# One weight load moved up, one unit of the output product moved up, and one pair of copies shared by two engines, in an attention-plus-MLP kernel

## The chip, the cores and the metric

The kernel runs on one core of a Trainium2 chip. The metric is the device time of one execution in microseconds; less is better. The engines are TensorE (PE, with its weight loads shown as PEld), VectorE (DVE), ScalarE (ACT), GpSimd (POOL) and SyncE (SP). Each takes its own instructions in order and waits on the others through semaphores. In this kernel nearly all loads from memory are issued by POOL, into one queue of software DMAs.

## The reference, cut to what matters

Two layers follow each other. The first is attention with an exponential decay per head (4 batches, 8 heads, 768 positions, 64 wide), computed in blocks of 64 positions with a running state. The second is an MLP on its 3072 x 512 output.

```
for each block b of 64 positions:
    intra = ((q_b k_b^T) * Dmask) v_b
    inter = (q_b * lam_pow) kv_state
    out_b = intra + inter
    kv_state = lam^64 * kv_state + (k_b * rev_pow)^T v_b

h = x @ w_in                      # 512 -> 2048
g = h + sin(alpha h)^2 / alpha
y = g @ w_out                     # 2048 -> 512
```

## The kernel before, in words

The 768 positions are cut into six chunks of 128. A chunk is taken for all four batches, so that the MLP works on 512 columns at a time. The batches go through the attention in two pairs: pair 0 is batches 0 and 1, pair 1 is batches 2 and 3. The order of the instructions on every engine is written out by hand; nothing reorders them.

**The MLP of a chunk.** `hidden(g, f)` multiplies one of 16 slices of `w_in` with the chunk's `xt` (four matmuls, L507), takes the sine on ACT (L510) and its square on ACT (L515) or DVE (L523). `finish(g, f)` forms the slice of `gall` on DVE (L524), and with that the PSUM bank of the slice is free. `project(g, m, part)` is one *unit*: four matmuls (L535) that multiply a quarter of `gall` for batch m with the quarter `w_out_sb[part]`. Units wait in a list, and `run(n)` issues the next n of it. The list for the first chunk begins (0,0), (1,0), (2,0), (3,0), (0,1), (1,1), (2,1), (3,1), (0,2), and so on, as (m, part). A unit with part 3 is followed by a store; the others are matmuls alone.

**The attention of the second chunk** is woven into the MLP of the first, and then into its last units. Its steps, which the change touches, are these.

- `turns_pair(t, nm, b, bk, engines)` turns k or q of a pair on PE (L338 to L341) into PSUM bank `bk`, both batches into the same bank. Two copies, one for each batch, take it from there into `QKT` (L344 for a copy on ACT, the DVE's own line where an engine given is `V`).
- `states(t, prs, ns)` forms the new state contributions of both 64-blocks of a pair (L423), block 0 in the first bank of `ns`, block 1 in the second.
- `update(1, 0, pr)` adds block 0 to the state on DVE (L399) and lets POOL cast it (L392). `update(1, 1, pr)` adds block 1 with four small DVE instructions (L403), and POOL casts it.
- `scores(t, prs, ns)` multiplies k and q (L443); `masks` takes the result out on DVE (L450).
- `outputs_first(t, prs, ns)` begins the outputs from the states (L457), block 0 in the first bank of `ns`, block 1 in the second. Its matmuls take the two blocks by turns. `outputs` adds the part within the block (L482), and `leave` takes the result to `xt` on DVE (L489).

For pair 1 the banks meet as follows: `states(1, (1,), (4, 2))` puts block 1 into bank 2, where L403 reads it; `outputs_first(1, (1,), (4, 2))` puts its own block 1 into bank 2.

A first chunk's helper, `turn_in_two`, has a form near to the changed one. It turns one batch of q into one bank and copies the first half on ACT (L296) and the second on DVE (L297).

**The loads** of the weights are issued by POOL: `load_w_in` (L89) and `load_w_out` (L92), 512 KB each as they land. On POOL's queue w_in's quarters 1, 2 and 3 are followed by w_out's first quarter; POOL's next instructions are the two decays of k for the first chunk (L257) and the table of masks (L217), and then the loads of the second chunk's k, q and v (L104).

Of the kernel before, what the change touches and what calls it, by code (L numbers as in the profile page):

```python
# [15 lines left out]
def kernel(  # L16
# [41 lines left out]
    def bank(nm, n, dtype=FP32):  # L58
        return psum.tile([P, 512 if dtype is FP32 else 1024], dtype, name=nm, tag=f"b{n}")
# [27 lines left out]
    def load_w_in(i, w0=0, w1=512):  # L87
        w = slice(512 * i + w0, 512 * i + w1)
        nc.gpsimd.dma_start(out=w_in_sb[i][:, :, w0:w1], in_=moe_w_in[:, w].rearrange("(c p) g -> p c g", p=P))  # L89

    def load_w_out(i):
        nc.gpsimd.dma_start(out=w_out_sb[i][:],  # L92
                            in_=moe_w_out[i * 512:(i + 1) * 512, :].rearrange("(f p) d -> p f d", p=P))

    def load(t, nm, b0, b1):
        dst, src = NAT[nm]
        to = dst[t][:, b0:b1, :, :].rearrange("p b h e -> p (b h) e")
        by_head = src[b0:b1, :, t * T:(t + 1) * T, :].rearrange("b h p e -> p (b h) e")
        n = H * (b1 - b0)
        if t > 1 and nm != "v" and b0 == 2:  # L100
            nc.gpsimd.dma_start(out=to[:, 0:n - 1, :], in_=by_head[:, 1:n, :])
            nc.gpsimd.dma_start(out=to[:, n - 1:n, :], in_=by_head[:, 0:1, :])
        else:
            nc.gpsimd.dma_start(out=to, in_=by_head)  # L104
# [20 lines left out]
        nc.gpsimd.dma_start(out=vn[0][:, 3, hs, :], in_=v[3, hs, 0:T, :].rearrange("h p e -> p h e"))  # L125
    load_w_in(0, 0, 2 * P)
    load_w_in(0, 2 * P, 512)
    for i in range(1, 4):
        load_w_in(i)

    fill = consts.tile([P, 512], BF16, name="fill")
    nc.vector.memset(fill[:], 1.0)  # L132
# [3 lines left out]
    def spin(n, bk, cols=256):  # L136
        ps = bank("hps", bk)
        for _ in range(n):
            nc.tensor.matmul(out=ps[:, 0:cols], lhsT=fill[:, 0:P], rhs=fill[:, 0:cols], start=True, stop=True)  # L139
# [82 lines left out]
    V, G, A = nc.vector, nc.gpsimd, nc.scalar  # L222
# [4 lines left out]
    def turned_by_one(t, pr):  # L227
        return bool(t) and pr == 1

    def in_turn(t, pr):  # L230
        return t > 1 and pr == 1
# [11 lines left out]
    def home(t, blk):  # L243
        return SB[2 if blk else t % 2]
# [7 lines left out]
    def decay_k(t, b0, b1):  # L252
        if t not in kdec:
            kdec[t] = kdp.tile([P, B, H, D], BF16, name="kdec")
        R = later["R64" if t else "R128"]
        o = int(in_turn(t, b0 // 2))
        nc.gpsimd.tensor_tensor(out=kdec[t][:, b0:b1, :, :], in0=kn[t][:, b0:b1, :, :],  # L257
                                in1=R[:, o:o + H].unsqueeze(1).unsqueeze(3).broadcast_to([P, b1 - b0, H, D]),
                                op=ALU.mult)
# [56 lines left out]
    def turn(t, nm, b, n, eng):  # L316
        src, u = (kn, 0) if nm == "k" else (qn, 1)
        ps = bank("T_ps", n, BF16)[:].rearrange("p (n c i) -> p n c i", n=2, c=HP)[:, u]
        for hp in range(HP):
            nc.tensor.transpose(out=ps[:, hp, :], in_=src[t][:, b, 2 * hp:2 * hp + 2, :], identity=iden[:])  # L320
        if eng is nc.scalar:
            eng.copy(out=both[t][:, u, b, :, :], in_=ps)
        else:
            eng.tensor_copy(out=both[t][:, u, b, :, :], in_=ps)
# [4 lines left out]
    def turns_pair(t, nm, b, bk, engines):  # L329
        src, n = (kn, 0) if nm == "k" else (qn, 1)  # L330
        ps = bank("T_ps", bk, BF16)[:].rearrange("p (u c i) -> p u c i", u=2, c=HP)
        flat = src[t][:, b:b + 2].rearrange("p b h d -> p (b h) d")
        o = int(turned_by_one(t, b // 2) and not in_turn(t, b // 2))
        for u in range(2):
            for hp in range(HP):
                h = u * H + 2 * hp + o
                if h + 2 <= 2 * H:
                    nc.tensor.transpose(out=ps[:, u, hp, :], in_=flat[:, h:h + 2, :], identity=iden[:])  # L338
                else:
                    nc.tensor.transpose(out=ps[LO, u, hp, :], in_=flat[:, h, :], identity=iden[:])  # L340
                    nc.tensor.transpose(out=ps[HI, u, hp, :], in_=flat[:, 0, :], identity=iden[:])  # L341
        for u, eng in enumerate(engines):
            if eng is nc.scalar:
                eng.copy(out=both[t][:, n, b + u, :, :], in_=ps[:, u])  # L344
            else:
                eng.tensor_copy(out=both[t][:, n, b + u, :, :], in_=ps[:, u])
# [29 lines left out]
    def states1(t, pr, n):  # L376
        ps = bank("KV0_ps", n)[:].rearrange("p (u c d) -> p u c d", u=2, c=HP)
        for h in range(2 * H):
            half, m = where(1, pr, h)
            nc.tensor.matmul(out=ps[halves(half), m // HP, m % HP, :], lhsT=head(kdec, t, pr, h),  # L380
                             rhs=vn[t][:, 2 * pr + h // H, h % H, :], start=True, stop=True)
        new_state(1, pr, ps, "first")
# [4 lines left out]
    def decay_state(n, pr):  # L387
        nc.gpsimd.tensor_tensor(out=pair(SD, pr), in0=pair(S_of[n], pr), op=ALU.mult,  # L388
                                in1=L64[:, pr].unsqueeze(1).unsqueeze(3).broadcast_to([P, 2, HP, D]))

    def cast_state(n, pr, dst):
        nc.gpsimd.tensor_copy(out=pair(dst, pr), in_=pair(S_of[n], pr))  # L392
# [42 lines left out]
    def scores(t, prs=BOTH, ns=None):  # L435
        banks_of("F", t, prs, ns, "F_ps")
        for pr in prs:
            for u in range(2):
                for hp in range(HP):
                    for blk in range(2):  # L440
                        for hd in range(2):
                            w = halves(blk)
                            nc.tensor.matmul(out=att["F", t, pr, hd][w, u, hp, :],  # L443
                                             lhsT=KT[t][halves(hd), 2 * pr + u, hp, w],
                                             rhs=QT[t][halves(hd), 2 * pr + u, hp, w], start=True, stop=True)
# [57 lines left out]
    def hidden(g, f, between=None):  # L503
        hps = bank("hps", H0[f] if g == 0 else (0, 5, 4, 2)[f] if g == 1 and f < 4 else AB[0] if g == 1 and f == 15 else AB[f + 1] if g == 2 and f < 2 else HB[(f + 2) % 3] if g == 1 else HB[(16 * g + f + 1) % 3])
        w = w_in_sb[f // 4]
        for c in range(NDC):
            nc.tensor.matmul(out=hps[:], lhsT=w[:, c, (f % 4) * P:(f % 4 + 1) * P],  # L507
                             rhs=xt[g][:, c, :], start=(c == 0), stop=(c == NDC - 1))
        s_sb = mlps.tile([P, GRP], BF16, name="s_sb")
        nc.scalar.activation(out=s_sb[:], in_=hps[:], func=ACTF.Sin, scale=alpha_sb[:, f:f + 1])  # L510
        if between:
            between()
        s2 = mlps.tile([P, GRP], BF16, name="s2")
        if squarer(g, f) is A:
            nc.scalar.activation(out=s2[:], in_=s_sb[:], func=ACTF.Square)  # L515
        elif squarer(g, f) is G:
            nc.gpsimd.tensor_tensor(out=s2[:], in0=s_sb[:], in1=s_sb[:], op=ALU.mult)
        hps_of[g, f] = (hps, s_sb, s2)
# [99 lines left out]
    outs(0, 3, 4, None, 1)  # L618
    nc.vector.reciprocal(out=r_sb[:], in_=alpha_sb[:])
    spin(3, 3)  # L620
    load_w_out(0)
    decay_k(0, 0, 2)
    decay_k(0, 2, 4)
    mask_table()
# [25 lines left out]
    def run(n):  # L650
        for _ in range(min(n, len(behind))):
            behind.pop(0)()
# [3 lines left out]
    for f in range(NFC):  # L656
        hidden(0, f)
        if f in (1, 10):
            states1(0, f // 10, 2 if f == 10 else 4)
        if f == 10:  # L660
            decay_k(1, 0, 2)
            decay_state(1, 0)
            cast_state(1, 0, home(1, 0))
            load(1, "q", 2, 4)
            load_w_out(2)
            load_w_out(3)
            load(2, "v", 0, 2)
        if f in (11, 12):
            run(1)
        if f == 12:  # L670
            turns_pair(1, "k", 0, 4, (A, A))
        if f == 13:
            turn(1, "q", 0, 2, V)
            turn(1, "q", 1, 3, V)
        if f == 14:
            scores(1, (0,), (4, 2))
            masks(1, 0)
        if f == 15:
            run(1)
            states(1, (0,), (4, 2))  # L680
            finish(0, 14)
            update(1, 0, 0)
        if f != 14:
            finish(0, f)
# [1 line left out]
    decay_state(1, 1)  # L686
    cast_state(1, 1, home(1, 0))
    update(1, 1, 0)
    run(2)
    turns_pair(1, "k", 2, 4, (A, A))  # L690
    run(1)
    outputs_first(1, (0,), (5, 0))
# [4 lines left out]
    states(1, (1,), (4, 2))  # L697
    update(1, 0, 1)
    run(1)
    turns_pair(1, "q", 2, 5, (A, A))  # L700
    load(2, "k", 0, 2)
    run(1)
    update(1, 1, 1)
# [110 lines left out]
```

## Time and profile before

| | us |
|---|---|
| median of 3 runs (207.2 to 207.66) | 207.48 |
| the profiled execution, its own time | 207.33 |
| its span, first to last instruction | 205.6 |
| PE busy in the span | 198.1 (96%) |
| ACT busy | 143.2 (70%) |
| DVE busy | 131.5 (64%) |
| POOL busy | 106.5 (52%) |

The span is what the trace covers; 1.73 us of the execution lie outside of it. Times inside the trace count from the span's start. The granted TensorE clock was 0.999 over the span.

In the timeline a row has the start, the time, the engine, the line and operation, out<-in by the names of the program, and the count; a bracket at the end is the idle time of the engine before it and what ended it. Rows of the same kind that follow each other are merged, and a few matmul records can be missing.

### The profile page before, as it was taken

Reading aid. Unit: us, or ns where it says so; the run is one execution under the profiler, and the core shown is the slowest. Engines: PE = TensorE matmul, PEld = TensorE weight load, DVE = VectorE, ACT = ScalarE, POOL = GpSimd, SP = SyncE. Lnnn points to the kernel's source line nnn. Section 1 sums busy time; section 2 is a strip of 40 time slices with the busy share of each in tenths; the row PEclk is TensorE's granted clock in tenths of the full one; section 3 lists DMA queues with packets and bytes.
Section 4 is the critical chain, followed back from the end, with each engine's and each line's share of the span. In section 5 each row is a group of like instructions: output and inputs, shape, how many; then the busy total and the mean of one; then the engine's idle time right before and its main releaser. Section 6 shows DMA issues by size and latency. Waiting matters only on the chain.

```text
span 205.6 us, 5385 instructions
## 1 busy us (share of the span) xinstructions
PE 198.1 (96%) x2235; PEld 98.3 (48%) x2265; DVE 131.5 (64%) x219; ACT 143.2 (70%) x241; POOL 106.5 (52%) x112
## 2 busy tenths in 40 slices
PE   7999989999999999999999999999999999999994
PEld 2764445554454444445444445444445444444443
DVE  7794979473889878967556967555967544444000
ACT  7798987224999799676776666776666787887121
POOL 8999939988979975999966930002000000000000
PEclk9999999999999999999999999999999999999999
DMA  8999999999989999899999929401101101110213
GB/s 132 170 178 205 203 162 176 189 176 154 150 275 105 128 151 184 82 150 155 152 149 155 181 64 192 117 3 51 54 0 54 51 0 54 53 51 0 104 51 105
DMA packets 96683, 24.49 MB, mean 119 GB/s; under 512 B 87938, under 2 KB 94226, under 8 KB 96658
## 3 DMA queue, kind: packets, MB, share of 16 engines
q0 software_dynamic: 74528, 13.37, 86.9%
q1 hardware_dynamic: 22128, 10.76, 25.5%
q8 instruction: 18, 0.29, 0.6%
q14 instruction: 7, 0.06, 0.1%
q10 hardware_dynamic: 2, 0.00, 0.0%
HBM read 27.27 MB, written 6.29 MB: 163 GB/s over the span
## 4 chain that ended last, share of the span: by engine, by line
PE 84%; DMA 7%; POOL 6%; issue 1%; ACT 1%; POOLq 0%; ACTq 0%
PE ops L535 39%; PE hps L507 35%; DMA w_out<-in_moe_w_out_dram 7%; PE O_ps L457 2%; POOL w_in L89 2%; PE hps L560 2%; PE F_ps L443 2%; PE KV_ps L423 2%; POOL kn L104 1%; PE O_ps L482 1%; POOL vn L104 1%; PE T_ps L338 1%; POOL qn L114 1%; POOL vn L125 1%; ACT QKT L344 1%
## 5 line engine op out<-in xcount | busy, mean ns | idle before, releaser
L524 DVE SCALAR_TENSOR_TENSOR gall<-s,r_sb,hps 128x512 bf16<-128x512 bf16 x96 | 71.1, 745 | 44.5 <-ACT s L515 44.3
L507 PE MATMUL hps<-xt,w_in 128*128 128x512 bf16 x369 | 94.3, 379 | 1.1 <-issue 0.3
L535 PE MATMUL ops<-w_out,gall 128*128 128x512 bf16 x353 | 90.4, 380 | 1.7 <-DMA w_out<-in_moe_w_out_dram 0.6
L510 ACT ACTIVATE s_sb<-hps,alpha_sb 128x512 bf16<-128x512 f32 x96 | 65.2, 684 | 32.0 <-PE hps L507 31.5
L515 ACT ACTIVATE s<-s_sb 128x512 bf16<-128x512 bf16 x91 | 57.3, 630 | 2.8
L507 PEld LDWEIGHTS <-w_in 128*128 128x128 bf16 x384 | 36.6, 98 | 42.8 <-DMA w_in<-in_moe_w_in_dram 0.3
L535 PEld LDWEIGHTS <-gall 128*128 128x128 bf16 x368 | 34.6, 98 | 41.5 <-DMA w_out<-in_moe_w_out_dram 1.1
L257 POOL TENSOR_TENSOR kdec<-kn,R 128x1024 bf16<-128x1024 bf16 x12 | 22.9, 1937 | 4.2 <-DMA kn<-in_k_dram 4.1
L392 POOL CAST sb<-S 128x512 bf16<-128x512 f32 x20 | 12.3, 621 | 21.3 <-DVE S L399 21.3
L388 POOL TENSOR_TENSOR SD<-S,L 128x512 f32<-128x512 f32 x16 | 16.8, 1050 | 8.6 <-DVE S L399 8.5
L489 DVE TENSOR_TENSOR xt<-O_ps,Etab 128x512 bf16<-128x512 f32 x20 | 12.8, 684 | 6.4 <-PE O_ps L482 6.4
L104 POOL DMA_DIRECT2D vn<-in_v_dram x13 | 14.7, 1137 | 0.0
L542 DVE COPY o_sb<-ops 128x512 f32<-128x512 f32 x15 | 10.3, 689 | 4.2 <-PE ops L535 4.2
L450 DVE TENSOR_TENSOR STm<-F_ps,C 128x512 bf16<-128x512 f32 x20 | 12.8, 683 | 0.3 <-PE F_ps L443 0.3
L544 ACT COPY o_sb<-ops 128x512 f32<-128x512 f32 x8 | 4.6, 576 | 12.0 <-PE ops L535 12.0
L399 DVE TENSOR_TENSOR S<-SD,KV_ps 128x512 f32<-128x512 f32 x16 | 10.8, 683 | 0.1
L104 POOL DMA_DIRECT2D kn<-in_k_dram x9 | 10.0, 1113 | 0.4 <-issue 0.3
L344 ACT COPY QKT<-T_ps 128x512 bf16<-128x512 bf16 x8 | 4.3, 586 | 5.3 <-PE T_ps L341 5.3
L139 PE MATMUL hps<-fill 128*128 128x256 bf16 (+1 forms) x24 | 6.5, 391 | 1.4 <-DVE fill L132 1.4
L104 POOL DMA_DIRECT2D qn<-in_q_dram x6 | 7.1, 1188 | 0.0
L457 PEld LDWEIGHTS <-sb 64*64 64x64 bf16 x320 | 4.3, 108 | 4.8 <-issue 4.7
L356 DVE TENSOR_TENSOR STm<-F_ps,C 128x512 bf16<-128x512 f32 x8 | 5.2, 686 | 0.8 <-PE F_ps L352 0.4
(92 smaller groups left out, 116.8 us busy)
## 6 DMA issues: line engine op xcount, KB each, us to landing
out_dram<-o_sb SPq DMA_DIRECT2D x19, 256.0 KB, 2.4
vn<-in_v_dram POOLq DMA_DIRECT2D x10, 256.0 KB, 7.9
w_out<-in_moe_w_out_dram POOLq DMA_DIRECT2D x4, 512.0 KB, 10.8
w_in<-in_moe_w_in_dram POOLq DMA_DIRECT2D x3, 512.0 KB, 9.4
kn<-in_k_dram POOLq DMA_DIRECT2D x6, 256.0 KB, 8.7
qn<-in_q_dram POOLq DMA_DIRECT2D x6, 256.0 KB, 8.5
out_dram<-o_sb SPq DMA_DIRECT2D x8, 128.0 KB, 1.8
kn<-in_k_dram POOLq DMA_DIRECT2D x4, 240.0 KB, 6.7
```

Of the source, the lines that this page charges most:

```text
L104: nc.gpsimd.dma_start(out=to, in_=by_head)
L257: nc.gpsimd.tensor_tensor(out=kdec[t][:, b0:b1, :, :], in0=kn[t][:, b0:b1, :, :], in1=R[:, o:o + H].unsqueeze(1).unsqueeze(3).broadcast_to ...
L388: nc.gpsimd.tensor_tensor(out=pair(SD, pr), in0=pair(S_of[n], pr), op=ALU.mult, in1=L64[:, pr].unsqueeze(1).unsqueeze(3).broadcast_to([P, ...
L392: nc.gpsimd.tensor_copy(out=pair(dst, pr), in_=pair(S_of[n], pr))
L399: nc.vector.tensor_tensor(out=S, in0=pair(SD, pr), in1=ps, op=ALU.add)
L450: nc.vector.tensor_tensor(out=st[:, hd], in0=att["F", t, pr, hd], op=ALU.mult, in1=of_mask(C64, t, pr, hd).unsqueeze(1).broadcast_to([P, 2 ...
L489: nc.vector.tensor_tensor(out=xview(t)[:, 2 * pr:2 * pr + 2, blk, :, :], in0=att["O", t, pr, blk], in1=Eb, op=ALU.mult)
L507: nc.tensor.matmul(out=hps[:], lhsT=w[:, c, (f % 4) * P:(f % 4 + 1) * P], rhs=xt[g][:, c, :], start=(c == 0), stop=(c == NDC - 1))
L510: nc.scalar.activation(out=s_sb[:], in_=hps[:], func=ACTF.Sin, scale=alpha_sb[:, f:f + 1])
L515: nc.scalar.activation(out=s2[:], in_=s_sb[:], func=ACTF.Square)
L524: nc.vector.scalar_tensor_tensor(out=gall[g][:, f, :], in0=s2[:], scalar=r_sb[:, f:f + 1], in1=hps[:], op0=ALU.mult, op1=ALU.add)
L535: nc.tensor.matmul(out=ops[:], lhsT=gall[g][:, f, m * P:(m + 1) * P], rhs=w_out_sb[part][:, f % 4, :], start=(f == 0), stop=(f == NFC - 1))
```

## The change

Three edits. The load of `w_out`'s first quarter is issued ahead of `w_in`'s last quarter. After the last slice of the first chunk's MLP, two units are run ahead of the second chunk's first states where there was one, and one is run behind them where there were two. Of the two copies of the last turned q (pair 1 of the second chunk), the second is given to DVE.

```diff
     load_w_in(0, 2 * P, 512)
-    for i in range(1, 4):
-        load_w_in(i)
+    load_w_in(1)
+    load_w_in(2)
+    load_w_out(0)
+    load_w_in(3)
...
     spin(3, 3)
-    load_w_out(0)
     decay_k(0, 0, 2)
...
         if f == 15:
-            run(1)
+            run(2)
             states(1, (0,), (4, 2))
             finish(0, 14)
             update(1, 0, 0)
...
     update(1, 1, 0)
-    run(2)
+    run(1)
     turns_pair(1, "k", 2, 4, (A, A))
     run(1)
...
     update(1, 0, 1)
     run(1)
-    turns_pair(1, "q", 2, 5, (A, A))
+    turns_pair(1, "q", 2, 5, (A, V))
     load(2, "k", 0, 2)
     run(1)
     update(1, 1, 1)
     scores(1, (1,), (5, 0))
```

On the engines this makes: on POOL two neighbouring issues change places; on PE four matmuls of unit (3,0) stand ahead of the 32 of the states; on ACT one copy is gone, and on DVE a copy stands between L399 of `update(1, 0, 1)` and the four L403 of `update(1, 1, 1)`. In the changed program that copy on DVE has one wait, for the count that ACT reaches with its own copy of the pair.

## The prediction

> **What bounds the kernel now.** First the page: what is busy, and how much room there is.
>
> ```profile
> span 205.6 us, 5385 instructions
> PE 198.1 (96%) x2235; PEld 98.3 (48%) x2265; DVE 131.5 (64%) x219; ACT 143.2 (70%) x241; POOL 106.5 (52%) x112
> ```
>
> TensorE is busy for 96% of the span, so only what PE waits for can be won, and whatever makes PE wait is lost. Next, therefore, the waits of PE, all of them:
>
> ```profile
> PE hps L139 <- DVE fill L132: 1.4, 1, 1.4
> PE ops L535 <- DMA w_out<-in_moe_w_out_dram: 0.6, 1, 0.6
> PE ops L535 <- issue: 0.5, 3, 0.2
> PE hps L507 <- issue: 0.3, 2, 0.2
> PE F_ps L443 <- ACT QKT L344: 0.2, 1, 0.2
> ```
>
> Two of these are what the change touches: 0.6 us for w_out's first quarter, and 0.2 us for the copies of the last turned q. The chain that ended last tells what lies behind the first, and the timeline of PE where it falls:
>
> ```profile
> 13.50 13.73 DMA w_out<-in_moe_w_out_dram
> 27.23 0.05 issue
> ```
>
> ```profile
> 25.61 1.04 PE L507 MATMUL hps<-xt,w_in 128*128 128x512 bf16 x4
> 27.28 1.04 PE L535 MATMUL ops<-w_out,gall 128*128 128x512 bf16 x4 [0.63 <-DMA w_out<-in_moe_w_out_dram]
> 28.15 1.03 PE L507 MATMUL hps<-xt,w_in 128*128 128x512 bf16 x4
> 29.88 0.61 PE L338 MATMUL T_ps<-iden,kn 128*128 128x128 bf16 x8
> 31.19 0.61 PE L320 MATMUL T_ps<-iden,qn 128*128 128x128 bf16 x8
> ```
>
> The load was issued at 13.50 and landed at 27.23; PE went on 0.05 later. Slices and units follow each other every 0.87 us (27.28 to 28.15), so the unit would have begun at 25.61 + 0.87 = 26.48. The wait is worth 27.28 - 26.48 = 0.80 us; the 0.63 in brackets counts from the end of the pipelined matmul. After that PE waits for nothing to the end of the span but the 0.2 and the few gaps of "issue", so a shift in this stretch reaches the end of the kernel whole.
>
> **Edit 1, the loads.** What stands in the queue ahead of w_out and behind it, from POOL's timeline, and the time from issue to landing of each, from the view of the DMAs:
>
> ```profile
> 12.77 0.84 POOL L89 DMA_DIRECT2D w_in<-in_moe_w_in_dram  x1
> 19.18 1.26 POOL L104 DMA_DIRECT2D kn<-in_k_dram  x1
> 20.39 1.20 POOL L104 DMA_DIRECT2D qn<-in_q_dram  x1
> ```
>
> ```profile
> w_in<-in_moe_w_in_dram POOLq DMA_DIRECT2D x1, 512.0 KB, 11.2
> kn<-in_k_dram POOLq DMA_DIRECT2D x1, 256.0 KB, 9.7
> qn<-in_q_dram POOLq DMA_DIRECT2D x1, 256.0 KB, 10.3
> ```
>
> The landings are 12.77 + 11.2 = 23.97 for w_in's last quarter, 27.23 for w_out's first, 19.18 + 9.7 = 28.88 for the second chunk's k and 20.39 + 10.3 = 30.69 for its q. They come in the order of issue. On POOL the two issues change places and nothing else is passed, so I let the two places keep their landings: w_out at 23.97, long before 26.48, and w_in at 27.23. That one is wanted by the slice that begins at 28.15, now 28.15 - 0.80 = 27.35: hidden by 0.12.
>
> Then what is late next. The k turn moves to 29.88 - 0.80 = 29.08, and k is there at 28.88. The q turn would move to 31.19 - 0.80 = 30.39, but q lands at 30.69 whatever PE does; with the same 0.05 it starts at 30.74. So the stall does not vanish. Of 0.80 us, 0.35 turn up again at q, and the gain past that point is 31.19 - 30.74 = 0.45.
>
> **Edit 2, the unit.** The next places in question, on PE and on DVE:
>
> ```profile
> 33.84 1.03 PE L535 MATMUL ops<-w_out,gall 128*128 128x512 bf16 x4
> 34.80 0.45 PE L423 MATMUL KV_ps<-vn,kdec 64*64 64x64 bf16 x32
> 35.18 1.90 PE L535 MATMUL ops<-w_out,gall 128*128 128x512 bf16 x8
> 36.91 0.55 PE L338 MATMUL T_ps<-iden,kn 128*128 128x128 bf16 x7
> ```
>
> ```profile
> 33.45 1.28 DVE L450 TENSOR_TENSOR STm<-F_ps,C 128x512 bf16<-128x512 f32 x2
> 35.36 0.69 DVE L399 TENSOR_TENSOR S<-SD,KV_ps 128x512 f32<-128x512 f32 x1
> ```
>
> The same matmuls in another order cost PE nothing. The states need the banks that the masks free: before at 33.45 + 1.28 = 34.73, with the states at 34.80, so with both 0.45 earlier they would still meet. The moved unit puts 0.87 between them: states at 34.80 - 0.45 + 0.87 = 35.22, done at 35.67. L399 can start at 35.72 and ends at 36.41, where it ended at 36.05 before. It frees bank 4 for the second k turn, which stands at 36.91 - 0.45 = 36.46, just as 36.41 + 0.05 comes. The slack is gone, and I take 0.03 off. Gain so far 0.42, edit 2 alone worth 0 (bounds -0.05 and +0.05). POOL's cast waits for L399, so it and the load behind it come up to 0.36 later. What hangs on these loads first is the third chunk's decay of k on POOL, and the states behind it on PE:
>
> ```profile
> 50.64 3.92 POOL L257 TENSOR_TENSOR kdec<-kn,R 128x1024 bf16<-128x1024 bf16 x2 [0.92 <-DMA kn<-in_k_dram]
> 56.31 0.73 PE L423 MATMUL KV_ps<-vn,kdec 64*64 64x64 bf16 x64
> ```
>
> The decay ends at 50.64 + 3.92 = 54.56, 1.75 before the states, which covers the 0.36; without that cover it would be lost on PE.
>
> **Edit 3, the copies.** First a form of it that the kernel already has, `turn_in_two`, from the timelines of ACT and DVE; then the place itself on ACT, DVE and PE, with the mean of one copy on ACT (586 ns), and a turned copy on DVE with the row after it.
>
> ```profile
> 6.76 0.37 ACT L296 COPY QKT<-T_ps 128x256 bf16<-128x256 bf16 x1 [0.27 <-PE T_ps L295]
> 7.17 0.29 DVE L297 COPY QKT<-T_ps 128x256 bf16<-128x256 bf16 x1 [0.59 <-ACT QKT L296]
> ```
>
> ```profile
> 42.48 1.07 ACT L344 COPY QKT<-T_ps 128x512 bf16<-128x512 bf16 x2 [3.00 <-PE T_ps L341]
> L344 ACT COPY QKT<-T_ps 128x512 bf16<-128x512 bf16 x8 | 4.3, 586 | 5.3 <-PE T_ps L341 5.3
> 31.95 0.42 DVE L324 COPY QKT<-T_ps 128x512 bf16<-128x512 bf16 x1
> 32.33 0.42 DVE L523 TENSOR_TENSOR s<-s_sb 128x512 bf16<-128x512 bf16 x1
> 42.68 1.12 DVE L403 SCALAR_TENSOR_TENSOR S<-S,L,KV_ps 128x128 f32<-128x128 f32 x4
> 43.60 0.45 PE L443 MATMUL F_ps<-QKT 64*64 64x64 bf16 x32 [0.20 <-ACT QKT L344]
> 43.88 0.67 PE L457 MATMUL O_ps<-QKT,sb 64*64 64x64 bf16 x31
> ```
>
> Two engines that copy out of one bank do not work side by side here: DVE sat idle for 0.59 and began at 7.17, 0.04 after ACT's copy was done (6.76 + 0.37 = 7.13). The changed program has the same wait on the new copy. So the halves run one after the other, as they do on ACT alone now, and the new wait stands at the head of DVE's queue. Behind it are the four L403, and behind those the masks.
>
> In times, with the gain of 0.42: ACT's copy from 42.48 - 0.42 = 42.06 to 42.65 (0.59 for one), DVE's from 42.69 to 43.11. The scores can start at 43.16, 0.44 earlier than 43.60; this alone would be a small gain over two copies on ACT. But L403 starts 0.38 after DVE's copy (31.95 to 32.33), at 43.07, where it started at 42.68; with 1.12 it ends at 44.19. L403 reads bank 2, and the second matmul of `outputs_first` writes bank 2. Now L403 ends at 42.68 + 1.12 = 43.80 and the outputs start at 43.88, with no idle time. After the change they would be due 0.28 behind the scores (43.60 to 43.88), at 43.44, and have to wait to 44.19 + 0.05 = 44.24: a new wait of 0.80 on PE, and a start 0.36 later than now. Against the gain of 0.42 edit 3 costs 0.78.
>
> The Trainium skill speaks against this edit: "PSUM — Partial Sum Buffer", section "PSUM bank collisions raise a hardware error", says that accesses of two engines to one bank in the same partitions, reads included, have to be kept apart by a semaphore. The trace agrees, by the 0.59. Its section "Specifications (TRN2)" lets ScalarE and VectorE read PSUM in parallel as long as the banks differ; by that, with a bank for each half, the sum would be that of the last rival below, and no run here shows it.
>
> **The sum.** -0.42 + 0.78 = +0.36 us. Against the profiled execution's 207.33 that is 207.69; the median of the runs stands 0.15 higher, at 207.48, and the forecast for a median is 207.48 + 0.36 = 207.84, 0.17% slower. About 0.2%, or 0.41 us, is what a measurement of this kernel can tell from no change.
>
> **The rivals.** *The early load gains less.* With g for the gain at the second q turn, the time changes by 0.78 - g, as the outputs then hang on ACT's copy. g is at most 0.45 by q's landing, and every place with little room (w_in's 0.12, k's 29.08 against 28.88, bank 4's 0.00) can only take from it; a w_in or q that lands 0.45 late in the other order leaves nothing. For it speaks that the margins are so thin, against it that the queue has been at work without a break and moves the same bytes. At g = 0 it is 207.48 + 0.78 = 208.26. From g below 0.37 on the change is measurably slower.
>
> *The outputs do not wait for L403.* The trace of before shows no such wait, only that the outputs began 0.08 after L403 was done. If bank 2 did not hold them up, PE would keep the gain of the scores, 0.42 to 0.44, and the time would be 207.48 - 0.42 = 207.06, faster. It decides once L403 ends later than 43.39. Against it is the code: the same bank number in `states` and `outputs_first`.
>
> *The halves run side by side.* DVE's copy then starts with ACT's at 42.06, and the outputs at 42.06 + 0.38 + 1.12 + 0.05 = 43.61, 0.27 earlier than 43.88: 207.48 - 0.27 = 207.21. Against it are the 0.59 and the wait in the program; for it only that the first form could have waited for something else.
>
> **The numbers.** The forecast's case, g between 0.25 and 0.45, has 0.62; it gives 207.81 to 208.01. Because all the thin margins work one way, I put 0.36 of it above 207.89 and 0.26 below. The small gain has 0.18, all slower; no wait for L403 has 0.10, faster; side by side has 0.10, within. That is faster 0.10, same 0.36, slower 0.54: the likeliest time lies just inside the bound, the weight just outside of it. The range goes from 207.2, where side by side ends, to 208.3 for g = 0 with the price of edit 3 a little high; left out is the case that is faster. The likeliest case's own range is 207.8 to 208.0.
>
> **What would show it.** Right: no wait of PE for w_out; in its place one of about 0.35 for q's load ahead of L320, with the turn at 30.74; DVE's new copy idle before it, released by ACT's copy at about 42.65; PE idle for some 0.8 ahead of L457, put down to DVE's L403; everything after 44 later by 0.36. Wrong: if w_in takes w_out's place among the waits, edit 1 failed; if DVE's copy starts with ACT's, the halves overlap; if L457 follows the scores without idle time, bank 2 was no bound. A wait anywhere behind 50 would mean that I missed a consumer.

## The result, and the profile after

| | before | after |
|---|---|---|
| median, us (7 runs each) | 207.48 | 208.20 |
| range of the runs | 207.15 to 207.82 | 207.97 to 208.65 |
| profiled execution, its own time | 207.33 | 208.3 |
| its span | 205.6 | 206.4 |

The change makes the kernel slower: the ratio is 1.0035, with a 95% interval of 1.0022 to 1.0048, or +0.72 us by the medians. The forecast was 207.84. Direction, wait and place came as predicted; the size is that of the first rival with no gain at all from edits 1 and 2 (208.26). One execution of edit 3 alone, at a granted clock of 0.759 (258.72 us), and one of the last kernel below (1012.11 us) count in no ratio here. Line numbers are each kernel's own: those named in the prediction, but for the loads, are two higher in after (the units are L537 for L535, the updates L405 for L403, the outputs L459 for L457), and a few kernels below have others again, so the names of out<-in are the safer guide.

First the page of after: what is busy.

```profile
span 206.4 us, 5385 instructions
PE 198.6 (96%) x2235; PEld 98.2 (48%) x2265; DVE 132.2 (64%) x220; ACT 142.6 (69%) x240; POOL 106.7 (52%) x112
```

Nothing shows here but one copy that went from ACT (241 instructions before, 240 now) to DVE (219 before, 220 now). The waits of PE in after tell more (in total, times, longest):

```profile
PE O_ps L459 <- DVE S L405: 0.6, 1, 0.6
PE ops L537 <- issue: 0.5, 3, 0.2
PE hps L509 <- issue: 0.3, 2, 0.2
PE ops L537 <- DVE gall L526: 0.2, 1, 0.2
PE F_ps L445 <- DVE QKT L348: 0.2, 1, 0.2
```

The 0.6 for w_out is gone, and a 0.6 ahead of the outputs from the states stands in its place. There is one wait that no step of the prediction named: 0.2 for `gall`. The timeline of PE in after, at the places that the prediction followed:

```profile
26.74 1.03 PE L537 MATMUL ops<-w_out,gall 128*128 128x512 bf16 x4
27.60 1.03 PE L509 MATMUL hps<-xt,w_in 128*128 128x512 bf16 x4
...
29.77 1.03 PE L509 MATMUL hps<-xt,w_in 128*128 128x512 bf16 x3
30.92 0.62 PE L322 MATMUL T_ps<-iden,qn 128*128 128x128 bf16 x8
...
33.75 1.89 PE L537 MATMUL ops<-w_out,gall 128*128 128x512 bf16 x8 [0.22 <-DVE gall L526]
35.57 0.45 PE L425 MATMUL KV_ps<-vn,kdec 64*64 64x64 bf16 x32
...
36.87 0.55 PE L340 MATMUL T_ps<-iden,kn 128*128 128x128 bf16 x7
...
43.69 0.45 PE L445 MATMUL F_ps<-QKT 64*64 64x64 bf16 x32 [0.17 <-DVE QKT L348]
43.97 0.19 PE L459 MATMUL O_ps<-QKT,sb 64*64 64x64 bf16 x1
44.72 0.66 PE L459 MATMUL O_ps<-QKT,sb 64*64 64x64 bf16 x30 [0.56 <-DVE S L405]
45.54 1.67 PE L537 MATMUL ops<-w_out,gall 128*128 128x512 bf16 x7 [0.16 <-issue]
```

The last of these rows in the kernel before:

```profile
44.71 1.67 PE L535 MATMUL ops<-w_out,gall 128*128 128x512 bf16 x7 [0.16 <-issue]
```

PE takes the unit for w_out's first quarter without a wait. But the second k turn, where 0.42 should have been won, starts at 36.87, against 36.91 before. Behind it PE loses time at the place of edit 3: the second matmul of the outputs starts at 44.72, and the units behind the outputs start at 45.54, 0.83 later than before. The timelines of DVE, ACT and POOL in after:

```profile
32.07 0.84 DVE L525 TENSOR_TENSOR s<-s_sb 128x512 bf16<-128x512 bf16 x1
...
36.13 0.69 DVE L401 TENSOR_TENSOR S<-SD,KV_ps 128x512 f32<-128x512 f32 x1 [0.58 <-PE KV_ps L425]
...
43.22 0.42 DVE L348 COPY QKT<-T_ps 128x512 bf16<-128x512 bf16 x1 [0.72 <-ACT QKT L346]
43.56 1.11 DVE L405 SCALAR_TENSOR_TENSOR S<-S,L,KV_ps 128x128 f32<-128x128 f32 x4
```

```profile
42.60 0.59 ACT L346 COPY QKT<-T_ps 128x512 bf16<-128x512 bf16 x1 [3.17 <-PE T_ps L343]
```

```profile
32.03 0.60 POOL L394 CAST sb<-S 128x512 bf16<-128x512 f32 x1
```

DVE sits idle for 0.72 ahead of its copy, which starts 0.03 after ACT's is done (42.60 + 0.59 = 43.19). L405 ends at 43.56 + 1.11 = 44.67, and the outputs go on 0.05 later. Further up, the square on DVE takes 0.84, where the same instruction took 0.42 before; POOL's cast, from 32.03 to 32.63, lies beside it. That row becomes the key to the missing gain.

### The profile page after: what moved, and what is told of

It reads as the page before. It is cut to its first block, busy times and chain, and to the rows that moved or that the text cites. A ratio compares the mean times of both kernels' runs of the same rounds, so it can differ in the third digit from the quotient of the medians.

```text
span 206.4 us, 5385 instructions
## 1 busy us (share of the span) xinstructions
PE 198.6 (96%) x2235; PEld 98.2 (48%) x2265; DVE 132.2 (64%) x220; ACT 142.6 (69%) x240; POOL 106.7 (52%) x112
## 4 chain that ended last, share of the span: by engine, by line
PE 83%; ACT 6%; issue 3%; DMA 2%; DVE 2%; POOL 2%; ACTq 0%; POOLq 0%
PE ops L537 37%; PE hps L509 34%; ACT s_sb L512 3%; DMA qn<-in_q_dram 2%; PE O_ps L459 2%; ACT s L517 2%; PE hps L562 2%; PE KV_ps L425 2%; POOL kn L104 1%; PE O_ps L484 1%; PE F_ps L445 1%; PE hps L141 1%; DVE gall L526 1%; PE T_ps L340 1%; PE O_ps L365 1%
## 5 line engine op out<-in xcount | busy, mean ns | idle before, releaser
L537 PE MATMUL ops<-w_out,gall 128*128 128x512 bf16 x353 | 90.3, 379 | 1.2 <-issue 0.5
L537 PEld LDWEIGHTS <-gall 128*128 128x128 bf16 x368 | 34.7, 98 | 40.8 <-issue 0.9
L452 DVE TENSOR_TENSOR STm<-F_ps,C 128x512 bf16<-128x512 f32 x20 | 12.8, 682 | 0.0
L401 DVE TENSOR_TENSOR S<-SD,KV_ps 128x512 f32<-128x512 f32 x16 | 10.8, 682 | 0.7 <-PE KV_ps L425 0.6
L346 ACT COPY QKT<-T_ps 128x512 bf16<-128x512 bf16 x7 | 3.8, 583 | 5.7 <-PE T_ps L343 5.7
L459 PEld LDWEIGHTS <-sb 64*64 64x64 bf16 x320 | 4.4, 108 | 5.4 <-issue 5.3
L459 PE MATMUL O_ps<-QKT,sb 64*64 64x64 bf16 x320 | 5.8, 195 | 0.6 <-DVE S L405 0.6
```

The costliest lines, as they stand in the source:

```text
L452: nc.vector.tensor_tensor(out=st[:, hd], in0=att["F", t, pr, hd], op=ALU.mult, in1=of_mask(C64, t, pr, hd).unsqueeze(1).broadcast_to([P, 2 ...
L459: nc.tensor.matmul(out=att["O", t, pr, blk][halves(h % 2), u, h // 2, :], lhsT=home(t, blk)[halves(half), 2 * pr + m // HP, m % HP, :], rh ...
L537: nc.tensor.matmul(out=ops[:], lhsT=gall[g][:, f, m * P:(m + 1) * P], rhs=w_out_sb[part][:, f % 4, :], start=(f == 0), stop=(f == NFC - 1))
```

## The experiments

A time is the median of 11 or 12 runs, compared with runs of the kernel before in the same session (207.52 to 207.72 by session). The theory at the start: edit 3 costs some 0.7 to 0.8 because the two copies share a bank, and edits 1 and 2 won less than 0.42 because something else in that stretch came late.

### Edit 1 alone

```diff
     load_w_in(1)
     load_w_in(2)
+    load_w_out(0)
     load_w_in(3)
...
-    load_w_out(0)
```

> Edit 1 alone (w_out's first quarter ahead of w_in's last; units and copies as before). Theory A (edit 3 costs 0.7 to 0.8 us, edits 1 and 2 gain up to 0.42, and the 0.25 us by which the changed kernel was late at its first slices is chance): 0.3 to 0.45 us faster than before, PE no longer waiting for w_out, a wait of about 0.35 us ahead of the q turn at L322. Theory B (the early load itself is the loss, by slower loads ahead of the first slices or a late w_in): 0.2 us slower or more, with the first slice late against the kernel before.

Measured: 207.62 against 207.61, ratio 1.0004 (0.9990 to 1.0018), so between 0.21 us gained and 0.37 lost. Its PE timeline where w_in and q are wanted, and the square and the cast on DVE and POOL:

```profile
27.73 1.04 PE L509 MATMUL hps<-xt,w_in 128*128 128x512 bf16 x4 [0.21 <-DMA w_in<-in_moe_w_in_dram]
...
31.23 0.62 PE L322 MATMUL T_ps<-iden,qn 128*128 128x128 bf16 x8 [0.26 <-DMA qn<-in_q_dram]
```

```profile
32.37 0.87 DVE L525 TENSOR_TENSOR s<-s_sb 128x512 bf16<-128x512 bf16 x1
```

```profile
32.36 0.60 POOL L394 CAST sb<-S 128x512 bf16<-128x512 f32 x1
```

The gain of theory A lies outside of the interval; a loss as in theory B is not shown either. The w_out stall is gone and its time is spent again. w_in's last quarter landed at 27.68, not 27.23, so its slice starts 27.73 - 26.49 = 1.24 behind the unit where 0.87 would do; the q turn, due at 29.94 + 0.87 = 30.81, starts at 31.23; the unit that waits for `gall`, behind a square of 0.87, starts 1.06 behind its slice (33.02 to 34.08). Counted by the starts, as the prediction did, these are 0.37, 0.42 and 0.19 us; the brackets count from the end of the last matmul on record.

### Edits 1 and 2

As above, with one of the two units from behind `update(1, 1, 0)` ahead of the states; both copies stay on ACT.

> Edits 1 and 2, both copies of the last turned q on ACT. Theory A: 0.3 to 0.45 us faster than before, within 0.1 us of edit 1 alone, and 0.7 to 0.8 us faster than the full change; L403's last instruction done before the outputs from the states begin, with no wait there. Theory B: no faster than before. A third theory C (the moved unit brings VectorE's square of slice 13 under a POOL instruction, where it took 0.84 instead of 0.42 us in the changed kernel): here also 0.84 and a wait of 0.2 us of PE for gall, so only 0.2 us faster than before.

Measured: 207.52 against 207.61, ratio 0.9999 (0.9987 to 1.0012), a gain of at most 0.27. The 0.42 of the forecast lies outside of both intervals. PE, DVE and POOL of this run:

```profile
30.92 0.62 PE L322 MATMUL T_ps<-iden,qn 128*128 128x128 bf16 x8
...
33.72 1.89 PE L537 MATMUL ops<-w_out,gall 128*128 128x512 bf16 x8 [0.18 <-DVE gall L526]
```

```profile
32.07 0.81 DVE L525 TENSOR_TENSOR s<-s_sb 128x512 bf16<-128x512 bf16 x1
```

```profile
32.00 0.60 POOL L394 CAST sb<-S 128x512 bf16<-128x512 f32 x1
```

The wait of 0.18 and the long square are there without edit 3, and edit 1 alone has them too, so the moved unit, which theory C blamed, is not their reason. Nor is the moved load the only way to them: edit 3 alone, with the old order of loads, shows them below.

### Edit 2 alone

```diff
-            run(1)
+            run(2)
             states(1, (0,), (4, 2))
...
-    run(2)
+    run(1)
     turns_pair(1, "k", 2, 4, (A, A))
```

> Edit 2 alone (unit moved ahead of the first states; loads and copies as before). Theory A: within 0.1 us of before, since the same matmuls stand in another order and the second k turn only loses its slack. Theory C: 0 to 0.2 us slower if VectorE's square of slice 13 meets a POOL instruction.

Measured: 207.65 against 207.61, ratio 1.0007 (0.9991 to 1.0022). By itself the unit brings nothing that can be told. In its profile w_out landed at 27.40 and was waited for (its unit started at 27.44, due at 25.56 + 0.87 = 26.43); the q turn and the square:

```profile
31.36 0.61 PE L320 MATMUL T_ps<-iden,qn 128*128 128x128 bf16 x8
```

```profile
32.48 0.53 DVE L523 TENSOR_TENSOR s<-s_sb 128x512 bf16<-128x512 bf16 x1
```

PE is late here, so the square issues behind most of the cast (32.12 to 32.72) and is held up by 0.11 only.

### Edit 3 alone, twice

```diff
-    turns_pair(1, "q", 2, 5, (A, A))
+    turns_pair(1, "q", 2, 5, (A, V))
```

> Edit 3 alone (second copy of the last turned q on DVE; loads and units as before). Theory A: 0.7 to 0.8 us slower than before, with PE waiting about 0.5 to 0.8 us for DVE's L403 ahead of the outputs from the states. Theory B: within 0.2 us of before.

Measured: 208.32 against 207.61, ratio 1.0028 (1.0014 to 1.0041), +0.58 us, between 0.29 and 0.85: theory A. The rows below come from one more run of the same kernel.

> Edit 3 alone once more, for a profile at the full granted clock. The theory: DVE's copy starts 0.04 after ACT's copy ends, the four updates end about 1.5 us after DVE's copy starts, and PE waits 0.6 to 0.8 us ahead of the outputs from the states; the copy of ACT itself starts as before, 42.5 counted from the same first slices. If instead the wait falls on the scores, the bank of the outputs was no bound.

Measured: 208.32 in this one run. Some of the waits of PE, and rows of PE and DVE, in its trace:

```profile
PE O_ps L457 <- DVE S L403: 0.6, 1, 0.6
PE hps L507 <- DMA w_in<-in_moe_w_in_dram: 0.5, 1, 0.5
```

```profile
26.13 1.04 PE L507 MATMUL hps<-xt,w_in 128*128 128x512 bf16 x4
27.14 1.04 PE L535 MATMUL ops<-w_out,gall 128*128 128x512 bf16 x4
...
31.05 0.61 PE L320 MATMUL T_ps<-iden,qn 128*128 128x128 bf16 x8
```

```profile
32.19 0.86 DVE L523 TENSOR_TENSOR s<-s_sb 128x512 bf16<-128x512 bf16 x1
...
43.37 0.42 DVE L346 COPY QKT<-T_ps 128x512 bf16<-128x512 bf16 x1 [0.56 <-ACT QKT L344]
```

Edit 3 brings the wait of 0.6 by itself. And the trace shows something about the kernel before: the order of its loads is the old one, yet PE hardly waits for w_out (27.14, due at 26.13 + 0.87 = 27.00). An earlier w_in quarter came late and had already taken 0.5. The stall of 0.80 that edit 1 was to remove is not in every execution. With it gone the q turn starts at 31.05, close behind q's landing, and the square takes 0.86 here too, without edit 1.

### The full change, with the four updates ahead of DVE's copy

```diff
+    new_state(1, 1, att["KV", 1, 1, 1], "fused")   # the four L405
     turns_pair(1, "q", 2, 5, (A, V))
...
-    update(1, 1, 1)
+    cast_state(1, 1, home(2, 0))
```

> The full change with DVE's four L403 of the last state put ahead of its copy of the turned q (POOL's cast stays where it was). Theory A (the outputs wait for L403, which stands behind a copy that waits for ACT): L403 ends near 43.8 instead of 44.7, the copy then near 44.1, the scores start about 0.45 us later than in the full change and the outputs follow without a wait for L403; 0.2 to 0.4 us faster than the full change, so 0.3 to 0.5 us slower than before. If L403 is not the bound: as slow as the full change or slower, 0.7 us and more over before.

Measured: 207.97 against 207.57, ratio 1.0022 (1.0013 to 1.0031). PE's rows:

```profile
44.40 0.45 PE L445 MATMUL F_ps<-QKT 64*64 64x64 bf16 x32 [0.74 <-DVE QKT L348]
44.67 0.67 PE L459 MATMUL O_ps<-QKT,sb 64*64 64x64 bf16 x31
```

This is theory A: 0.46 slower than before, and 1.0035 - 1.0022 = 0.13%, or 0.27 us, faster than the full change. The wait for L405 is gone, and the scores wait for the copy instead, 0.74. Whichever goes first on DVE, the copy and the updates are one after the other ahead of the outputs.

### The full change, with the two batches of q in two banks

```diff
-    turns_pair(1, "q", 2, 5, (A, V))
+    turns_two_banks(1, 2, (5, 0), (A, V))   # one batch to a bank
```

> The full change with the two batches of the last turned q turned into two banks (5 and 0) instead of one, so that DVE's copy waits for PE and not for ACT. Theory A (one bank is why the halves run one after the other): DVE's copy starts within 0.1 us of ACT's, L403 ends near 44.1, the outputs come about 0.6 us earlier than in the full change; within 0.2 us of before. Rival: the two copies disturb each other anyway, or L403 is not the bound: 0.4 us slower than before or more.

Measured: 207.53 against 207.57, ratio 1.0001 (0.9988 to 1.0015), faster than the full change by 1.0035 - 1.0001 = 0.34%, or 0.71 us. ACT, DVE and PE:

```profile
42.11 0.58 ACT L364 COPY QKT<-T_ps 128x512 bf16<-128x512 bf16 x1 [2.65 <-PE T_ps L358]
```

```profile
41.84 0.68 DVE L419 TENSOR_TENSOR S<-SD,KV_ps 128x512 f32<-128x512 f32 x1
42.52 0.42 DVE L366 COPY QKT<-T_ps 128x512 bf16<-128x512 bf16 x1
```

```profile
44.03 0.66 PE L477 MATMUL O_ps<-QKT,sb 64*64 64x64 bf16 x30 [0.18 <-DVE S L423]
```

DVE's copy starts at 42.52, while ACT's runs to 42.69. It was expected within 0.1 of ACT's start and comes 0.41 behind it, because DVE has its own L419 to end first (41.84 + 0.68 = 42.52); it no longer waits for ACT. The shared bank, and the wait on ACT that the program has with it, is thus what sets the copies one behind the other, and nearly all of edit 3's price hangs on it. Even so the shared copy wins nothing that can be told: with both copies on ACT the ratio was 0.9999, here 1.0001. By this the trace bears out the Trainium skill, "PSUM — Partial Sum Buffer", section "Specifications (TRN2)", which lets the two engines read in parallel from different banks.

### The full change, with a unit between scores and outputs

```diff
     scores(1, (1,), (5, 0))
     masks(1, 1)
     load(2, "k", 2, 4)
+    run(1)
     outputs_first(1, (1,), (4, 2))
...
-    run(2)
+    run(1)
     outputs(1, (1,))
```

> The full change with one of the two units that follow the last outputs-from-states put ahead of them, behind the scores, so that PE has 0.87 us of work while DVE's L403 runs. Theory A: the wait of 0.56 us for L403 goes and the time falls to within 0.15 us of before, 0.5 to 0.7 us under the full change. If another wait takes its place (the masks ahead of the outputs within the block): a gain of less than 0.3 us.

Measured: 207.75 against 207.57, ratio 1.0012 (1.0003 to 1.0021). The copies are still one after the other, but PE has four matmuls to do meanwhile:

```profile
44.30 1.04 PE L537 MATMUL ops<-w_out,gall 128*128 128x512 bf16 x4
45.27 0.69 PE L459 MATMUL O_ps<-QKT,sb 64*64 64x64 bf16 x31
```

No wait ahead of L459. So the 0.56 there was PE's own loss and could be covered: 0.0023, or 0.48 us, come back. That is a little less than expected (0.5 to 0.7, to within 0.15 of before; it stays 0.25 above).

### Edits 1 and 2, with the square of slice 13 on ACT

```diff
-            return V if f in (3, 5, 7, 9, 13) else A
+            return V if f in (3, 5, 7, 9) else A
```

> Edits 1 and 2 with the square of slice 13 on ACT instead of DVE (copies of q both on ACT). In the runs with edit 1 that square took 0.81 to 0.87 us on DVE instead of 0.42 and ended 0.28 us after POOL's cast in each. Theory D (edit 1's gain is lost because the earlier square meets the cast, and q's landing takes the rest): no wait of PE for gall ahead of the unit, and 0.2 us faster than edits 1 and 2 with the square on DVE, so about 0.2 us under before. Rival: the lost gain is all in the landing of k and q; then within 0.1 us of edits 1 and 2.

Measured: 207.53 against 207.57, ratio 0.9992 (0.9982 to 1.0003). The wait for `gall` is gone, but in this profile w_in's early quarters came some 0.8 late, and the q turn started at 31.62. From the q turn to the second k turn it took 5.77 (the table below). But with the turn 0.37 behind q's landing the square on DVE would hardly have been held up either (edit 2 alone, 0.35 behind, took 5.77 with it). So neither the time nor this trace decides between theory D and its rival.

### Versions meant to beat both

From these readings: edits 1 and 2, q's first turn behind slice 14 in place of 13 (so that its load has landed), and no square on DVE there. The scores and masks of pair 0 and `finish(0, 13)` move with the turn.

```diff
-        if f == 13:
+        if f == 14:
             turn(1, "q", 0, 2, V)
             turn(1, "q", 1, 3, V)
-        if f == 14:
+            finish(0, 13)
+        if f == 15:
             scores(1, (0,), (4, 2))
             masks(1, 0)
-        if f == 15:
             run(2)
...
-        if f != 14:
+        if f not in (13, 14):
             finish(0, f)
...
-            return V if f in (3, 5, 7, 9, 13) else A
+            return V if f in (3, 5, 7, 9) else A
```

> Edits 1 and 2 with both turned copies on ACT, the first turn of the second chunk's q moved behind slice 14 of the first chunk (it stood behind slice 13), and the square of slice 13 on ACT in place of DVE. The theory: the stall of 0.80 us at w_out came back because the q turn stood 0.05 behind q's landing (30.9 to 31.2) and because DVE's square of slice 13 was held up by POOL's cast. With the turn one slice later (about 31.3) and no square on DVE there, neither remains; the next late things are the landings of the third chunk's loads and bank 4 at the second k turn. Expected: no wait ahead of the q turn and none for gall; the second k turn at 36.4 to 36.6 counted from slices that start as in the profile before; time 0.2 to 0.4 us below before, 207.2 to 207.4. The rival: what is gained is taken by something else, for one thing the chance spread of the first landings or the bank of the states; then the time is within 0.1 us of before.

Measured: 207.54 against 207.72, ratio 0.9991 (0.9976 to 1.0005): 0.18 below by the medians, less than the 0.2 to 0.4 expected. The next one adds the two banks of the sixth and the unit of the seventh experiment, and was run twice.

> The kernel of the run before, and with it the last turned q in two banks with one copy on ACT and one on DVE, and one unit of the output product between the scores and the outputs from the states. The theory: the second copy no longer waits for the first, and the unit covers the four updates of block 1, so neither the scores nor the outputs wait; against the run before it the 0.2 us ahead of the scores is gone. Expected: no wait ahead of scores or outputs, time 0.4 to 0.6 us below before, 207.0 to 207.2. The rival: the places are bound by landings, not by these copies; then it equals the run before within 0.1 us.

> The kernel of the run before once more, since its runs left the interval wide (0.9972 to 1.0017, median 207.28 against 207.72). The theory: neither q's landing, nor the held up square, nor the copies are late there, so it is 0.3 to 0.5 us faster than before, a ratio of 0.9976 to 0.9986 with an interval that ends below 1. The rival: the low median was chance, and the ratio lies between 0.9995 and 1.0005.

Measured: 207.28 against 207.72, ratio 0.9994 (0.9972 to 1.0017), and 207.35 against 207.52, ratio 0.9989 (0.9975 to 1.0003). PE in the first of the three and in the second:

```profile
31.58 0.61 PE L322 MATMUL T_ps<-iden,qn 128*128 128x128 bf16 x8
...
36.62 0.56 PE L340 MATMUL T_ps<-iden,kn 128*128 128x128 bf16 x7
```

```profile
43.26 0.44 PE L463 MATMUL F_ps<-QKT 64*64 64x64 bf16 x32
43.64 1.04 PE L555 MATMUL ops<-w_out,gall 128*128 128x512 bf16 x3
44.61 0.69 PE L477 MATMUL O_ps<-QKT,sb 64*64 64x64 bf16 x31
```

The waits in question are gone: the second k turn starts 0.29 earlier than before, and neither scores nor outputs wait. All three medians lie below before, by 0.17 to 0.44 us, but every interval reaches past 1, and the second run of the last kernel misses the interval below 1 that its theory asked for. Counted run by run they lean one way: 10 of the 12 runs of the first kernel and 18 of the 23 of the last lie under their session's median of before. So that these versions are faster than the kernel before is likely and not shown. They do beat the changed kernel.

## Why the prediction was right, and where it was off

**The sum** was -0.42 + 0.78 = +0.36; measured is +0.72. The range of the likeliest case, 207.8 to 208.0, missed 208.20; the whole range holds it only because it was drawn out to g = 0. Edit 3 was sized well: 0.78 predicted; by the runs 0.58 alone, and 1.0035 - 0.9999 = 0.36%, or 0.75 us, between the full change and edits 1 and 2. From the second k turn to the units behind the outputs the traces have 7.80 before and 8.50 with edit 3 alone, 7.95 with edits 1 and 2 and 8.67 with all three: 0.70 and 0.72 for edit 3. The trace of after follows the steps: from the start of ACT's copy to the outputs 44.24 - 42.06 = 2.18 was predicted, and 44.72 - 42.60 = 2.12 came. The small slip is that the first matmul of the outputs (block 0) went at 43.97; only from the second on did bank 2 hold them up. That the halves don't overlap, and that L403 holds up the outputs, both hold; the two rivals that denied it fell.

**The term that was mis-sized is g, the gain of edits 1 and 2: 0.42 predicted.** The runs give 1.0004 and 0.9999 for it, nothing that can be told from no gain, and the trace of after 36.91 - 36.87 = 0.04. The failing step is "0.80 - 0.35 = 0.45", taken from one profiled execution, with the margins behind it left as they were. That execution was a lucky pick: of the 108 runs of before beside the experiments only 14 took its 207.33 or less. A table from the traces shows two losses (q's landing is issue plus time to landing; times in us).

| kernel | q lands | q turn | second k turn | q turn to k turn | square on DVE |
|---|---|---|---|---|---|
| before | 30.70 | 31.19 | 36.91 | 5.72 | 0.42 |
| edit 2 alone | 31.01 | 31.36 | 37.13 | 5.77 | 0.53 |
| edit 3 alone | 30.98 | 31.05 | 37.19 | 6.14 | 0.86 |
| after | 30.88 | 30.92 | 36.87 | 5.95 | 0.84 |
| edit 1 alone | 31.18 | 31.23 | 37.38 | 6.15 | 0.87 |
| edits 1 and 2 | 30.88 | 30.92 | 36.84 | 5.92 | 0.81 |
| edits 1 and 2, square on ACT | 31.25 | 31.62 | 37.39 | 5.77 | none |
| q turn later | 31.13 | 31.58 | 36.62 | 5.04, a slice less | none |

*First, q's landing is the floor, and it moves.* With edit 1 the q turn starts 0.04 or 0.05 after q is there, but for the last two rows (in one w_in's early quarters came 0.8 late, in the other the turn stands a slice later). The 0.05 was right and the landing was not: it spreads over half a microsecond, and the profile of before had the earliest, 30.70. w_in's last quarter, which was to be hidden by 0.12, landed between 26.83 (after) and 27.68 (edit 1 alone) and held PE up in the second. What edit 1 can win is the distance from landing to turn in a kernel without it, less 0.05: 0.44, 0.30 and 0.02 in the three traces. The forecast's 0.45 was the top of that.

*Second, a q turn close behind q's landing runs the DVE square into POOL's cast.* POOL's decay of k waits for k's landing and the cast comes behind it, so the cast stays where the loads put it: it starts 1.09 to 1.18 after q's landing in the six traces of the table that have this square. Slice 13's square moves with PE: it starts 1.12 to 1.15 after the q turn. So a turn that follows the landing at once sends the square into the whole cast. The cast in the kernel before:

```profile
31.79 0.60 POOL L392 CAST sb<-S 128x512 bf16<-128x512 f32 x1
```

There the q turn stood 0.49 behind the landing; the square began at 32.33, 0.06 ahead of the cast's end at 32.39, and took its 0.42. With the turn 0.35 behind (edit 2 alone) it took 0.53, and 0.04 to 0.07 behind it took 0.81 to 0.87. In these five its end lies 0.28 to 0.29 after the cast's end (after: 32.07 + 0.84 = 32.91, and 32.03 + 0.60 = 32.63; edit 1 alone: 33.24 and 32.96; edits 1 and 2: 32.88 and 32.60; edit 2 alone: 33.01 and 32.72). The traces of the fifth to seventh experiment show the same: 0.80 to 0.87, with 0.28 to 0.29 behind the cast. So of the 0.45 at the q turn little could have reached the square's end even in the execution that the forecast was made from: by this distance the square could end at 32.39 + 0.28 = 32.67 (an estimate), and it ended at 32.75.

The delay passes to `finish(0, 13)`, to the unit that waits for `gall` and, where the unit is not moved, through the masks to the states, whose row then takes 0.68 in place of 0.45 (edit 1 alone and edit 3 alone). The Trainium skill, "SBUF — State Buffer", section "Summary: rules for kernel authors", has a rule for it: a DVE instruction with two inputs from SBUF and a GpSimd instruction that reads SBUF exclude each other, and the second to issue waits for the first. The fixed distance to the cast's end agrees with that; that it is 0.28 and not the 0.42 of a whole square suggests that a part of the instruction passes beside the cast, as far as the recorded end of the cast can be trusted. That the held up square costs time is read from these traces; no run here isolates it.

Both together give the size: the second k turn was forecast at 36.91 - 0.42 = 36.49 and came at 36.87, 0.38 late. Of this 30.92 - 30.74 = 0.18 is q's landing. Another 0.17 is the wait for `gall`: the unit starts 33.75 - 32.71 = 1.04 behind its slice in place of 0.87 (the bracket says 0.22 because the slice's fourth matmul is not on record). The last 0.03 is bank 4, which had no slack, as forecast: L401 ended at 36.13 + 0.69 = 36.82 and the k turn followed 0.05 later, 0.93 behind its unit in place of 0.87; the forecast had taken off 0.03 for this.

**Edit 2 at nothing** holds where the square is free or nearly so (5.77 against 5.72). Where it is held up, the moved unit gives the states' banks time to come free: 5.92 with it, 6.15 without. The prediction had only the first case.

**The rivals.** "The early load gains less" is what happened, with its chance of 0.18, and its 208.26 is near the 208.20. The reasons that it gave were part of it only: thin margins and a late landing, yes; that DVE and POOL would collide was not in it. Of the signs listed, the missing wait for w_out, DVE's copy released by ACT's, the wait by L403 and nothing behind 50 were right. The wait for q was there (in after the turn was due at 29.77 + 0.87 = 30.64 and started 0.28 later), at 30.92 and not at 30.74; that it is near the 0.35 is luck, since PE came to this stretch 0.25 late (25.86 against 25.61) and q landed 0.18 late. ACT's copy ended at 43.19 and not at 42.65, and everything after 44 was later by 0.83 and not by 0.36.

**Left open:** why landings spread by half a microsecond between executions of nearly the same code, whether the long square is the rule in the kernel before (its one trace lacks it, and both others with the old order of loads have it, in part or whole), and a gap of 0.16 between two matmuls of the last q turn in some traces, after and edits 1 and 2 among them (0.72 for its row where before has 0.55), which the profile puts down to nothing. In those two it takes what little the second k turn had won.

## What to carry to other kernels

A stall seen in one profiled execution was worth no more here than the distance to the next landing, and that landing, at the end of a long queue, was a spread of half a microsecond and not a time: take it from several executions before working with margins of 0.05 us. When PE moves up in time, list which instructions of other engines move with it and which are pinned to a load, and see what these two groups now run into. Sharing a copy between two engines cost 0.58 to 0.75 us here in one bank, where it puts the first copy's time into the other engine's queue, ahead of everything there; with a bank for each it cost nothing, and won nothing that could be told.

## What the runs showed of the hardware that was not expected

A `TENSOR_TENSOR` of 0.42 us on DVE (128x512, bf16, both inputs in SBUF) took 0.80 to 0.87 when it started up to 0.08 behind the start of a 0.60 us cast on POOL, 0.53 when it started 0.24 before the cast's end, and its usual 0.42 when it started 0.06 before it; in all but the last it ended 0.28 to 0.29 after the cast. Two copies from two PSUM banks on ACT and DVE kept their 0.58 and 0.42 side by side.
